# Three plain chunks instead of four, then halves of 448 columns, with part of the softmax on ScalarE

## The chip, the cores and the metric

One core of a Trainium2 chip runs the whole kernel. The metric is the device time of one execution in microseconds: 953.92 us is the median of 3 runs of the kernel before (953.56 to 955.15). PE is TensorE, PEld its weight loads, DVE is VectorE, ACT is ScalarE, POOL is GpSimd, SP is SyncE.

## The reference

Sliding-window attention over 8 batches, 8 heads, 576 positions of width 64, then a gated feed-forward layer on the 4608 x 512 result:

```python
scores = scale * np.matmul(q, k.transpose(0, 1, 3, 2))
mask_plain = (rel >= 0) & (rel < 32)                       # heads 0 to 3
mask_dil = (rel >= 0) & (rel < 128) & (rel % 4 == 0)       # heads 4 to 7
scores = np.where(masks, scores, -1000000000.0)
scores = scores - np.max(scores, axis=-1, keepdims=True)
attn = np.exp(scores)
attn = attn / (np.sum(attn, axis=-1, keepdims=True) + 1e-09)
x = matmul(attn, v)   # brought to [4608 tokens, 512]
g = x @ w_gate        # 512 x 1536
silu = g * (1.0 / (1.0 + np.exp(-g)))
out = (silu * (x @ w_val) @ w_out)                         # 1536 x 512
```

## The kernel before, in words

Tokens are cut into 12 chunks of 384 (`CH`). Attention works on packs: a pack is a pair of heads in a chunk, so there are 48, m = 0 to 47, four to a chunk. Each query block of 32 sees only 64 keys, so a pack is three or four groups of 128 queries by 64 keys for two heads.

A pack is handled in two visits, placed by the table `visit` (filled by `visits`) between the matmul groups of the feed-forward layer. Visit A of pack m (`attend`) issues the value matmuls of pack m - 1 (`results`), the score matmuls of m, then on DVE the normalising of m - 1 (`norm`) and the mask sum, maximum and subtraction of m (`shift`), on ACT the exponential (`exps`), and the loads of later packs on ACT's queue. Visit B transposes the normalised result of m - 1 (`turn_y`) and the exponentials of m (`turn_e`) on PE, copies both out of PSUM on ACT, and so gives four packs' worth of x for a chunk. Both visits use the one PSUM tile `two`.

The feed-forward layer has three parts. Every fp32 operand is split into a rounded high part and a rest (both float32r), and a product is high x high + high x low + low x high, three matmuls.

- Plain stage: the first 4 chunks (`NPLAIN`), each in 12 steps s over blocks of 128 of the 1536 columns. A step is 12 gate matmuls into `bank_g`, 12 value matmuls into `bank_v` (`gv_mm`), and 12 output matmuls of the step before (`out_mm`). ACT takes the tanh (`act_tanh`), DVE two products (`dve_u`, `dve_h`), ACT the high part (`h_hi`), POOL the rest (`h_lo`). During the first chunk the weights are loaded and decoded from 64-bit words.
- Mixing: in steps 12 to 47 sums and differences of weight blocks are made for the last stage (18 mixes, one for each i and `which`): `mix_parts` and `mix_sums` on DVE, a cast on ACT, `mix_low` on DVE, then four DMA to the DRAM tile `pieces` (`mix_out`); unmixed blocks go there directly (`plain_parts`).
- Halved stage: the other 8 chunks, two at a time (ci = 0 to 3). A pair is multiplied as 2 x 2 blocks with seven products instead of eight. `x_step` makes the seven x operands from the four quarters of x (two halves of tokens b11/b12, b21/b22) for the next pair at the end of the pair before; `gate_val` does 6 matmuls for each of 7 products, 6 blocks, gate and value; `gated` combines them; `h_split` makes the seven hidden operands; `outs` does 3 matmuls for each of 7 products, 6 blocks, 2 rows; `out_done` stores. The weight pieces come back from DRAM through a ring of 10 buffers (`ask`, on POOL's queue). The line L739 is every matmul of this stage, L698 is every subtraction or sum made through the helper `tt`.

The order of instructions on an engine is not that of the text: a scheduler of the framework places each instruction where it expects it ready, by program order as priority; `issue_after` and `manual_schedule` bind it in places. Within an engine the placed order is then kept.

## Time and profile before

| | |
|---|---|
| median of the runs | 953.92 us |
| profiled execution | 953.3 us |
| its span | 951.4 us |
| PE busy | 939.0 us |
| DVE busy | 653.7 us |
| ACT busy | 406.6 us |
| POOL busy | 376.8 us |
| DMA, mean over the span | 250 GB/s |

Busy time is the union of an engine's instructions in one profiled execution. Matmuls are pipelined: a row's mean duration (336 ns for 384 columns) is longer than the distance between the starts of two, and it is the distance that fills the span.

### The profile page before, as it was taken

How to read it: one execution, taken by the hardware profiler on the slowest of the kernel's cores; microseconds unless marked ns; L12 is line 12 of the kernel's file. 1: busy time of each engine (PE TensorE's matmuls, PEld its weight loads, DVE VectorE, ACT ScalarE, POOL GpSimd, SP SyncE). 2: the span in 40 equal slices, each digit the busy share in tenths (PEclk: the TensorE clock that was granted, in tenths of full speed). 3: DMA queues.
4: the chain of work that ended last, by engine and by line, in shares of the span. 5: the costliest groups of instructions: out<-in, count | busy, mean ns of one | idle time of the engine just before them, and what ended most of it. 6: DMA issues, size and time to landing. Idle time of an engine off the chain costs nothing.

```text
span 951.4 us, 23933 instructions
## 1 busy us (share of the span) xinstructions
PE 939.0 (99%) x9960; PEld 914.2 (96%) x9960; DVE 653.7 (69%) x1168; ACT 406.6 (43%) x788; POOL 376.8 (40%) x460
## 2 busy tenths in 40 slices
PE   7899999999999999999999999999999999999998
PEld 5799999999999999999999999999999999999998
DVE  4766557677667654776887677789487779466583
ACT  4886322333334223434454344446334446234352
POOL 1766311211111222343276334366244448354472
PEclk9999999999999999999999999999999999999999
DMA  9975164665766882989888988888989878988873
GB/s 368 339 281 188 43 218 154 241 205 201 240 233 224 270 293 70 279 272 297 270 271 275 330 287 258 270 254 291 350 262 297 244 237 281 309 245 261 250 235 120
DMA packets 86060, 238.12 MB, mean 250 GB/s; under 512 B 8768, under 2 KB 29120, under 8 KB 85952
## 3 DMA queue, kind: packets, MB, share of 16 engines
q0 software_dynamic: 36288, 132.14, 44.5%
q1 hardware_dynamic: 36848, 65.07, 19.4%
q10 hardware_dynamic: 12816, 39.38, 12.3%
q8 instruction: 79, 1.29, 0.5%
q14 instruction: 29, 0.24, 0.1%
HBM read 194.08 MB, written 42.47 MB: 249 GB/s over the span
## 4 chain that ended last, share of the span: by engine, by line
PE 93%; DVE 4%; ACT 2%; issue 1%; DMA 0%; ACTq 0%; DVEq 0%
PE bo L739 31%; PE bg L739 11%; PE bv L739 11%; PE bo L465 10%; PE bv L428 10%; PE bg L428 10%; PE two L366 3%; PE two L326 3%; PE two L350 2%; PE two L384 2%; DVE at_float32r L698 1%; DVE at_float L698 0%; DMA at_bfloat<-masks 0%; ACT at_float32r L246 0%; ACT at_int L207 0%
## 5 line engine op out<-in xcount | busy, mean ns | idle before, releaser
L739 PE MATMUL bo<-at_float32r,at_float32r 128*128 128x384 f32 x1728 | 318.6, 336 | 0.0
L739 PEld LDWEIGHTS bo<-at_float32r,at_float32r 128*128 128x128 f32 x1728 | 299.7, 188 | 1.1
L671 POOL DMA_DIRECT2D at_float32r<-pieces x252 | 137.8, 547 | 245.0 <-PE bo L739 140.5
L698 DVE TENSOR_TENSOR at_float<-bo,at_float 128x384 f32<-128x384 f32 x224 | 122.2, 553 | 101.7 <-PE bo L739 52.4
L457 POOL TENSOR_TENSOR at_float32r<-at_float,at_float32r 128x384 fp32r<-128x384 f32 x48 | 55.6, 1158 | 216.5 <-PE bo L465 169.5
L739 PE MATMUL bg<-at_float32r,at_float32r 128*128 128x384 f32 x648 | 137.0, 336 | 0.0
L739 PE MATMUL bv<-at_float32r,at_float32r 128*128 128x384 f32 x648 | 136.4, 336 | 0.0
L739 PEld LDWEIGHTS bv<-at_float32r,at_float32r 128*128 128x128 f32 x648 | 114.0, 188 | 0.5
L739 PEld LDWEIGHTS bg<-at_float32r,at_float32r 128*128 128x128 f32 x648 | 113.7, 188 | 0.7
L428 PE MATMUL bg<-at_float32r,at_float32r 128*128 128x384 f32 x576 | 111.5, 340 | 2.1 <-DVE at_float L442 1.4
L728 ACT CAST at_float32r<-at_float 128x384 fp32r<-128x384 f32 x168 | 82.9, 513 | 66.8 <-PE bv L739 22.7
L698 DVE TENSOR_TENSOR at_float32r<-at_float,at_float32r 128x384 fp32r<-128x384 f32 (+1 forms) x112 | 99.1, 908 | 17.9 <-ACT at_float32r L728 14.0
L428 PE MATMUL bv<-at_float32r,at_float32r 128*128 128x384 f32 x576 | 110.8, 339 | 0.0
L465 PE MATMUL bo<-at_float32r,at_float32r 128*128 128x384 f32 x576 | 109.4, 337 | 0.0
L698 POOL TENSOR_TENSOR at_float32r<-at_float,at_float32r 128x384 fp32r<-128x384 f32 x84 | 91.6, 1091 | 43.9 <-ACT at_float32r L728 42.8
L428 PEld LDWEIGHTS bg<-at_float32r,at_float32r 128*128 128x128 f32 x576 | 100.3, 188 | 3.9 <-POOL at_float32r L250 1.1
L428 PEld LDWEIGHTS bv<-at_float32r,at_float32r 128*128 128x128 f32 x576 | 100.4, 188 | 0.9
L465 PEld LDWEIGHTS bo<-at_float32r,at_float32r 128*128 128x128 f32 x576 | 100.4, 188 | 0.5
L765 ACT ACTIVATE at_float<-at_float 128x384 f32<-128x384 f32 x96 | 50.6, 527 | 99.4 <-DVE at_float L698 92.3
L442 DVE SCALAR_TENSOR_TENSOR at_float<-at_float,bg 128x384 f32<-128x384 f32 x48 | 26.6, 554 | 77.6 <-ACT at_float L437 77.6
L744 ACT COPY at_float<-bg 128x384 f32<-128x384 f32 x84 | 40.1, 478 | 81.4 <-PE bg L739 81.2
L698 DVE TENSOR_TENSOR at_float<-at_float,at_float 128x384 f32<-128x384 f32 (+1 forms) x64 | 54.6, 878 | 25.1 <-POOL at_float32r L698 11.3
(80 smaller groups left out, 987.8 us busy)
## 6 DMA issues: line engine op xcount, KB each, us to landing
at_float32r<-pieces POOLq DMA_DIRECT2D x252, 512.0 KB, 4.8
pieces<-at_float32r SPq DMA_DIRECT2D x126, 256.0 KB, 3.3
at_int<-w SPq DMA_DIRECT2D x24, 768.0 KB, 6.1
at_float<-vb ACTq DMA_DIRECT2D x36, 390.0 KB, 5.2
out<-at_float SPq DMA_DIRECT2D x48, 192.0 KB, 4.1
at_float<-qkb ACTq DMA_DIRECT2D x14, 448.0 KB, 6.1
at_float<-qkb ACTq DMA_DIRECT2D x15, 400.0 KB, 5.5
at_float<-qkb ACTq DMA_DIRECT2D x7, 640.0 KB, 7.0
```

Source lines behind the costliest of these rows:

```text
L326: nc.tensor.matmul(out=two[BQ * j:BQ * j + BQ, h, a + BK * g:a + BK * g + BK], lhsT=t[r, q:q + BQ], rhs=t[r, k:k + BK], start=not masked, ...
L366: nc.tensor.matmul(out=two[BQ * j:BQ * j + BQ, h, (D + 1) * g:(D + 1) * (g + 1)], lhsT=t[r, BQ * i:BQ * i + BQ], rhs=v[r, i, :], start=Tru ...
L428: nc.tensor.matmul(out=bank[:, :CH], lhsT=wcol(f, o, low), rhs=x[ORDER[j]], start=n == 0, stop=n == len(ops) - 1)
L442: last["h"] = nc.vector.scalar_tensor_tensor(out=t, in0=t, scalar=1.0, in1=bank_g[:, :CH], op0=ALU.add, op1=ALU.mult)
L457: nc.gpsimd.tensor_tensor(out=hl, in0=hst[i][0], in1=hst[i][1], op=ALU.subtract)
L465: nc.tensor.matmul(out=bank_o[j][:, :CH], lhsT=wcol(f, 2 * DM + P * j, low), rhs=x, start=f == 0 and low == 0 and x is hh, stop=f == NF - ...
L671: nc.gpsimd.dma_start(out=taken[asked], in_=pieces[asked % NPIECE])
L698: engine.tensor_tensor(out=out, in0=a, in1=b, op=op)
L728: nc.scalar.copy(out=o[:, 0], in_=src)
L739: nc.tensor.matmul(out=bank, lhsT=w, rhs=x, start=first and n == 0 and t in FRESH, stop=last and n == len(ops) - 1, skip_group_check=True)
L744: nc.scalar.copy(out=kept[KEPT[t]][r], in_=banks[0][r][:, :CH])
L765: nc.scalar.activation(out=f, in_=g, func=AF.Tanh, scale=0.5)
```

## The change

There are three plain chunks. The remaining 9 chunks of tokens are worked through in four pairs of halves, 448, 448, 448 and 384 wide (`HCS`), whose starts no longer coincide with the chunks of attention. So a pack's x goes out in pieces (`x_copies`), and what belongs to the pair after the one being filled goes to a spill buffer and is copied back later (`x_spilt`). The first difference of x is made in place of its first quarter (`x1 = b11`), and the two differences of hidden blocks are made in place on POOL after the first split. The buffers are laid out anew: the ring of pieces has 9, the hidden splits run 8 ahead, not 10.

In packs 9 to 23 (`by_group`) DVE only scales the maximum; ACT subtracts it as the bias of the exponential, one instruction for each group and head (64 columns), and does the division by the sum the same way. The 24 packs that the first pair needs now stand in three chunks' steps. The 18 mixes stand in steps 12 to 32, in four named places of a step, with two output buffers. Plain chunks are stored from ACT's queue, not SP's.

```diff
-NPLAIN = 4
+NPLAIN = 3
+HCS = (448, 448, 448, 384)
+HM = max(HCS)
...
+    def by_group(m):
+        return 8 < m < 24
...
+        if by_group(m):
+            nc.vector.tensor_scalar(out=mx, in0=mx, scalar1=-0.125, scalar2=None, op0=ALU.mult)
+            st[m]["bias"] = mx
+            return
         nc.vector.tensor_tensor(out=ev, in0=s, in1=mx.unsqueeze(3).broadcast_to([P, 2, ng, BK]), op=ALU.subtract)
...
+        for g in range(pk(m).ng):
+            for h in range(2):
+                nc.scalar.activation(out=e[:, g, h], in_=e[:, g, h], func=AF.Exp, scale=0.125,
+                                     bias=st[m]["bias"][:, h, g:g + 1])
...
+        if by_group(m):
+            for g in range(ng):
+                for h in range(2):
+                    nc.scalar.activation(out=y[:, g, h], in_=s[:, h, g, :D], func=AF.Copy, scale=z[:, h, g:g + 1])
+            return
...
-            nc.sync.dma_start(out=out[P * j:P * j + P, CH * ci:CH * ci + CH], in_=ot)
+            nc.scalar.dma_start(out=out[P * j:P * j + P, CH * ci:CH * ci + CH], in_=ot)
...
+    for n in range(8):
+        visits(9 + n, NB + 2 + 4 * n, NB + 5 + 4 * n)
+        visits(17 + n, SB - 38 + 4 * n, SB - 35 + 4 * n)
...
+    for m in range(32, NPK + 1):
+        a = SB + NSLOT * (m // 8 - 3) - 32 + (m % 8 > 0) * 6 + 15 * (m % 8)
         visits(m, a, a + 7)
...
+    mix_at = {NF + n * 20 // (3 * NP - 1): n for n in range(3 * NP)}
...
-    NAT = 10
+    NAT = 9
...
+        if ci > 0:
+            steps = [steps[k] for k in (0, 2, 6, 8, 3, 4, 5, 1, 7, 9, 10)]
...
         act_tanh(s)
+        mix_one(mix_high, mix_at.get(s - 1), "t")
         attend(3 * s)
         dve_u(s)
-        mix_to(2 * (s - NF) + 1)
+        plain_to(s - 10)
+        mix_one(mix_low, mix_at.get(s - 1), "h")
+        mix_one(mix_out, mix_at.get(s - 1), "w")
+        mix_one(mix_parts, mix_at.get(s), "h")
...
         dve_h(s)
+        mix_one(mix_sums, mix_at.get(s), "h")
         h_hi(s)
```

How it moves instructions, at three places. First PE in the halved stage, gate and value matmuls of one block (`bg`, `bv`, `bo` are the PSUM banks; the last field is partitions x columns). Before:

```order
L739 MATMUL bv<-at_768_float32r,at_1024_float32r 128x384 x6
L739 MATMUL bo_503<-at_768_float32r,at_1024_float32r 128x384 x6
L739 MATMUL bo_507<-at_768_float32r,at_1024_float32r 128x384 x6
L739 MATMUL bg<-at_768_float32r,at_1024_float32r 128x384 x6
L739 MATMUL bv<-at_768_float32r,at_1024_float32r 128x384 x6
```

Of the change:

```order
L799 MATMUL bv<-at_896_float32r,at_1024_float32r 128x448 x6
L799 MATMUL bo_503<-at_896_float32r,at_1024_float32r 128x448 x6
L799 MATMUL bo_507<-at_896_float32r,at_1024_float32r 128x448 x6
L799 MATMUL bg<-at_896_float32r,at_1024_float32r 128x448 x6
L799 MATMUL bv<-at_896_float32r,at_1024_float32r 128x448 x6
```

The sequence is the same, each matmul is 64 columns wider; 2268 matmuls have 448 columns and 2052 have 384, where 4752 had 384.

Second ACT in the plain stage, from one visit of a pack to the next (L356 and L381 copy the keys' transposes, L403 and L436 the high part of x, L437 and L488 are the tanh, L452 and L503 the cast `h_hi`, L629 and L680 the mixing's cast, L346 and L370 the exponential, L406 the scaling). Before:

```order
L308 DMA at_780_float_891<-vb 128x780
L302 DMA at_1280_float_516<-qkb 128x800
L452 CAST at_384_float32r<-at_384_float_586 128x384
L346 ACTIVATE at_384_float_887<-at_384_float_887 128x384
L629 CAST at_2048_float32r<-at_1024_float_518 128x4x256
L437 ACTIVATE at_384_float_630<-bg 128x384
L452 CAST at_384_float32r<-at_384_float_630 128x384
L356 COPY at_384_float_954<-two 128x384
L403 CAST at_384_float32r<-two 128x384
```

Of the change:

```order
L318 DMA at_780_float_884<-vb 128x780
L312 DMA at_1280_float_516<-qkb 128x896
L406 ACTIVATE at_384_float_1078<-two,at_6_float_298 128x64 x6
L503 CAST at_384_float32r<-at_384_float_623 128x384
L488 ACTIVATE at_384_float_579<-bg 128x384
L680 CAST at_2048_float32r<-at_1024_float_518 128x4x256
L370 ACTIVATE at_384_float_880<-at_384_float_880,at_6_float_237 128x64 x6
L503 CAST at_384_float32r<-at_384_float_579 128x384
L381 COPY at_384_float_947<-two 128x384
L436 CAST at_384_float32r<-two 128x384
```

Twelve instructions of 64 columns stand where one of 384 stood, and the exponentials stand behind a tanh and a mixing cast.

Third PE in the same stretch, from the matmuls ahead of a pack's visit B to its transposes, in the change from the scores (L341) on (L384 and L414 transpose the result, L350 and L375 the exponentials). Before:

```order
L465 MATMUL bo_511<-at_384_float32r,at_1536_float32r 128x384
L465 MATMUL bo_515<-at_384_float32r,at_1536_float32r 128x384
L428 MATMUL bg<-at_384_float32r,at_1536_float32r 128x384 x12
L428 MATMUL bv<-at_384_float32r,at_1536_float32r 128x384 x12
L384 MATMUL two<-at_256_float_59,at_384_float_1085 128x128 x3
L350 MATMUL two<-at_256_float_59,at_384_float_887 128x128 x3
L465 MATMUL bo_503<-at_384_float32r,at_1536_float32r 128x384 x2
```

Of the change:

```order
L341 MATMUL two<-at_1280_float_516 32x64 x24
L516 MATMUL bo_507<-at_384_float32r,at_1536_float32r 128x384
L516 MATMUL bo_511<-at_384_float32r,at_1536_float32r 128x384
L516 MATMUL bo_515<-at_384_float32r,at_1536_float32r 128x384
L479 MATMUL bg<-at_384_float32r,at_1536_float32r 128x384 x12
L479 MATMUL bv<-at_384_float32r,at_1536_float32r 128x384 x12
L414 MATMUL two<-at_256_float_59,at_384_float_1078 128x128 x3
L516 MATMUL bo_503<-at_384_float32r,at_1536_float32r 128x384 x2
L375 MATMUL two<-at_256_float_59,at_384_float_880 128x128
L516 MATMUL bo_507<-at_384_float32r,at_1536_float32r 128x384 x2
L375 MATMUL two<-at_256_float_59,at_384_float_880 128x128
```

The transposes of the exponentials, three in a piece before, now stand one by one between output matmuls.

## Rows read from the trace of the kernel before

**Rows 1.** The page, busy time, share of the span and instructions of each engine.

```profile
PE 939.0 (99%) x9960; PEld 914.2 (96%) x9960; DVE 653.7 (69%) x1168; ACT 406.6 (43%) x788; POOL 376.8 (40%) x460
```

**Rows 2.** The chain that ended last, whole span, shares by engine and line.

```profile
by line: PE bo L739 30.7%; PE bg L739 11.3%; PE bv L739 11.3%; PE bo L465 10.2%; PE bv L428 10.2%; PE bg L428 10.1%; PE two L366 2.8%; PE two L326 2.5%; PE two L350 1.6%; PE two L384 1.5%; DVE at_float32r L698 1.2%; issue 0.8%; DVE at_float
```

**Rows 3.** Two windows: PE, PEld, DVE, ACT, POOL busy us; clock, DMA share, GB/s.

```profile
150.00:340.00 190.00, 190.00 (x2329) 185.09 (x2328) 133.10 (x261) 61.81 (x113) 34.52 (x35) 1.00 0.68 231
400.00:900.00 500.00, 499.93 (x4952) 491.39 (x4951) 364.15 (x645) 220.80 (x460) 234.57 (x328) 1.00 0.88 277
```

**Rows 4.** PE's timeline, halved stage: start us, us, what; first and eleventh group.

```profile
798.45 0.69 PE L739 MATMUL bv<-at_float32r,at_float32r 128*128 128x384 f32 x3
...
803.65 0.68 PE L739 MATMUL bv<-at_float32r,at_float32r 128*128 128x384 f32 x3
```

**Rows 5.** Groups of instructions by form, PE: count, busy us, mean ns, idle before.

```profile
L739 PE MATMUL bo<-at_float32r,at_float32r 128*128 128x384 f32 x1728 | 318.6, 336 | 0.0
...
L739 PE MATMUL bg<-at_float32r,at_float32r 128*128 128x384 f32 x648 | 137.0, 336 | 0.0
...
L428 PE MATMUL bg<-at_float32r,at_float32r 128*128 128x384 f32 x576 | 111.5, 340 | 2.1 <-DVE at_float L442 1.4 <-POOL at_float32r L250 0.8
```

**Rows 6.** The same view, DVE: a step's product, mixing, softmax.

```profile
L442 DVE SCALAR_TENSOR_TENSOR at_float<-at_float,bg 128x384 f32<-128x384 f32 x48 | 26.6, 554 | 77.6 <-ACT at_float L437 77.6
...
L632 DVE TENSOR_TENSOR at_float32r<-at_float,at_float32r 128x1024 fp32r<-128x1024 f32 x18 | 23.6, 1313 | 7.0 <-ACT at_float32r L629 7.0
...
L341 DVE TENSOR_TENSOR at_float<-at_float,at_float 128x384 f32<-128x384 f32 x34 | 20.7, 608 | 0.6
L377 DVE TENSOR_TENSOR at_float<-two,at_float 128x384 f32<-128x384 f32 x36 | 20.1, 557 | 1.2
...
L340 DVE TENSOR_REDUCE at_float<-at_float 128x6 f32<-128x384 f32 x34 | 18.7, 551 | 0.9
L338 DVE TENSOR_TENSOR at_float<-two,at_bfloat 128x384 f32<-128x384 f32 x34 | 18.6, 548 | 0.0
...
L619 DVE TENSOR_TENSOR at_float<-at_float32r 128x512 f32<-128x512 f32 x24 | 15.4, 684 | 0.0
...
L619 DVE TENSOR_TENSOR at_float<-at_float32r 128x256 f32<-128x256 f32 x24 | 8.6, 418 | 0.0
L627 DVE TENSOR_TENSOR at_float<-at_float 128x256 f32<-128x256 f32 x18 | 8.5, 470 | 0.5
...
L375 DVE TENSOR_SCALAR at_float<-two 128x6 f32<-128x6 f32 x36 | 5.7, 158 | 14.9 <-PE two L326 14.9
```

**Rows 7.** The same view, ACT: tanh, exponential, mixing's cast, copy out of PSUM.

```profile
L437 ACT ACTIVATE at_float<-bg 128x384 f32<-128x384 f32 x48 | 23.5, 489 | 62.6 <-PE bg L428 58.1 <-DMA at_float<-vb 4.5
...
L346 ACT ACTIVATE at_float<-at_float 128x384 f32<-128x384 f32 x40 | 20.9, 523 | 36.0 <-DVE at_float L341 36.0
L629 ACT CAST at_float32r<-at_float 128x1024 fp32r<-128x1024 f32 x18 | 18.9, 1049 | 19.4 <-DVE at_float L628 19.0 <-DMA pieces<-at_float32r 0.4
L356 ACT COPY at_float<-two 128x384 f32<-128x384 f32 x36 | 17.2, 478 | 14.8 <-PE two L350 13.9
...
L346 ACT ACTIVATE at_float<-at_float 128x512 f32<-128x512 f32 x8 | 5.1, 632 | 8.3 <-DVE at_float L341 8.3
```

**Rows 8.** Timelines of DVE and of POOL in the plain stage.

```profile
150.21 0.56 DVE L442 SCALAR_TENSOR_TENSOR at_float<-at_float,bg 128x384 f32<-128x384 f32 x1 [1.50 <-ACT at_float L437]
150.68 1.22 DVE L632 TENSOR_TENSOR at_float32r<-at_float,at_float32r 128x1024 fp32r<-128x1024 f32 x1
...
159.82 2.02 DVE L632 TENSOR_TENSOR at_float32r<-at_float,at_float32r 128x1024 fp32r<-128x1024 f32 x1 [1.25 <-ACT at_float32r L629]
...
159.74 1.01 POOL L457 TENSOR_TENSOR at_float32r<-at_float,at_float32r 128x384 fp32r<-128x384 f32 x1 [5.30 <-PE bo L465]
```

**Rows 9.** Timelines near the end of the second pair: DVE, then PE.

```profile
650.54 8.12 DVE L698 TENSOR_TENSOR at_float32r<-at_float,at_float32r 128x768 fp32r<-128x768 f32 x7
...
661.96 0.55 PE L350 MATMUL two<-at_float,at_float 128*128 128x128 f32 x3
```

More of the change, by code (lines that the diff above doesn't have):

```diff
@@ L36 @@
 BK = 2 * BQ
-NPLAIN = 4
-CC = 2 * CH
+NPLAIN = 3
+HCS = (448, 448, 448, 384)
+HM = max(HCS)
+STARTS = [CH * NPLAIN + 2 * sum(HCS[:n]) for n in range(len(HCS) + 1)]
 NT = 7
@@ L109, in attention_moe @@
     NCH = out.shape[1] // CH
+    NC = len(HCS)
+    assert STARTS[NC] == out.shape[1]
     NS = NPLAIN * NF
@@ L405, in x_copies, with x_spilt @@
         else:
-            x = x32_first[k // 2] if c == NPLAIN else x32[k // 2][c % 2]
-            src, x = x_views(m, bank, x[:, k % 2, :])
-            nc.scalar.copy(out=x, in_=src)
-        st[m].clear()
+            n = len(SEGMENTS[c % 3]) if pk(m).ng * P > CH else 1
+            ahead = sum(CH * c >= x for x in STARTS)
+            for g in range(n):
+                a, t, left = pk(m).ng * P // n * g, CH * c + CH // n * g, CH // n
+                while left:
+                    ci = sum(t >= x for x in STARTS) - 1
+                    h, r = divmod(t - STARTS[ci], HCS[ci])
+                    w = min(left, HCS[ci] - r)
+                    x = x32[k // 2][h][:, k % 2, r:r + w]
+                    if ci == ahead:
+                        x = spill[k // 2][:, k % 2, r:r + w]
+                        spilt[ci] = max(spilt.get(ci, 0), r + w)
+                    nc.scalar.copy(out=x, in_=bank[:, a:a + w])
+                    a, t, left = a + w, t + w, left - w
+        st[m].clear()
+    def x_spilt(ci):
+        n = spilt.pop(ci, 0)
+        if n:
+            for a in range(2):
+                nc.scalar.copy(out=x32[a][0][:, :, :n], in_=spill[a][:, :, :n])
     def x_copy_hi(m, bank):
@@ L436, in act_tanh @@
         t = t_ring()
[L437 removed]
+        last["t"] = nc.scalar.activation(out=t, in_=bank_g[:, :CH], func=AF.Tanh, scale=0.5)
         hst[i] = [t, None, None]
@@ L640, in mix_out, with mix_one, plain_to @@
             last["w"] = nc.sync.dma_start(out=pieces[p, :, o:o + 4 * P], in_=t[:, k].rearrange("p l c -> p (l c)"))
-    mixed = 0
-    def mix_stage():
-        nonlocal mixed
-        n, stage = divmod(mixed, 3)
-        mixed += 1
-        if n < 3 * NP:
-            with tc.issue_after(last["h"].ins):
-                (mix_parts, mix_sums, mix_low)[stage](n)
-            with tc.issue_after(last["w"].ins):
-                if stage == 0:
-                    plain_parts(*divmod(n, 3))
-                elif stage == 2:
-                    mix_out(n)
-    NAT = 10
+    mix_at = {NF + n * 20 // (3 * NP - 1): n for n in range(3 * NP)}
+    def mix_one(what, n, behind):
+        if n is not None:
+            with tc.issue_after(last[behind].ins):
+                what(n)
+    plain = 0
+    def plain_to(n):
+        nonlocal plain
+        while plain < min(n, 3 * NP):
+            with tc.issue_after(last["w"].ins):
+                plain_parts(*divmod(plain, 3))
+            plain += 1
     taken = {}
     asked = 0
-    NC = (NCH - NPLAIN) // 2
     def ask(n):
@@ L740, in products, with keep, total @@
                              stop=last and n == len(ops) - 1, skip_group_check=True)
-    def keep(t, r):
+    def keep(t, r, hc):
         if t in KEPT:
-            nc.scalar.copy(out=kept[KEPT[t]][r], in_=banks[0][r][:, :CH])
-    def total(t, r, ring):
+            nc.scalar.copy(out=kept[KEPT[t]][r][:, :hc], in_=banks[0][r][:, :hc])
+    def total(t, r, ring, hc):
         _, b, k = SUMS[t]
-        o = ring()
-        tt(nc.vector, o, banks[b][r][:, :CH], kept[k][r], ALU.add)
+        o = ring()[:, :hc]
+        tt(nc.vector, o, banks[b][r][:, :hc], kept[k][r][:, :hc], ALU.add)
         return o
@@ L786, in out_done @@
             a, b = SUMS[t][0]
-            o = total(t, r, o_ring)
-            row, col = P * (2 * a + r), CH * (NPLAIN + 2 * ci + b)
-            nc.sync.dma_start(out=out[row:row + P, col:col + CH], in_=o)
-    def mix_to(half):
-        while mixed < half * 9 * NP // 62:
-            mix_stage()
+            o = total(t, r, o_ring, HCS[ci])
+            row, col = P * (2 * a + r), STARTS[ci] + HCS[ci] * b
+            nc.sync.dma_start(out=out[row:row + P, col:col + HCS[ci]], in_=o)
     for s in range(NS):
```

149 lines of the change are left out of this document (76 added, 73 removed).

## The prediction

> **What bounds the kernel now.** I read the page's busy shares first, then the chain of waits, then two windows, then single lines. The page has TensorE (PE) busy for 939.0 of 951.4 us [rows 1], and the chain that ended last, followed back, runs through PE matmuls for over 90% of the span: 83.8% in the big matmuls of L739, L428 and L465 together, 8.4% (2.8 + 2.5 + 1.6 + 1.5) in the attention's small ones, 79.9 us for 44 packs, 1.8 us each [rows 2]. In the plain stage (150 to 340 us) PE is busy for 190.00 of 190.00 us while VectorE (DVE) has 133.10 (70%) and ScalarE (ACT) 61.81; in the halved stage (400 to 900 us) PE has 499.93 of 500, DVE 364.15, ACT 220.80 [rows 3]. The granted clock is 1.00 in both, the 2.4 GHz level. So the time is the number of matmuls times their spacing, and every other engine matters only where PE has to wait for it. The spacing is in the timeline: ten groups of three L739 matmuls start between 798.45 and 803.65, 5.20 us for 30, 173.3 ns each [rows 4]. 384 columns at 2.4 GHz are 160.0 ns, so 13.3 ns lie beside the columns. The counts are 1728 + 648 + 648 = 3024 in the halved stage and 576 each of gate, value and output, 1728, in the plain one [rows 5] (the value's and the plain output's rows have the same counts).
>
> **The change: fewer, wider matmuls.** A plain chunk takes 12 x 36 = 432 matmuls, a halved one 7 x 6 x 2 x 6 + 7 x 6 x 2 x 3 = 756. Before: 4 x 432 + 4 x 756 = 4752, all of 384 columns. After: 3 x 432 + 756 = 2052 of 384, and 3 x 756 = 2268 of 448. So 432 go: 432 x 0.1733 = -74.9 us. 2268 grow by 64 columns. The trace has no matmul of 448 columns, so the price is bounded. Below: the columns alone, 448 / 2.4 = 186.7 ns, +13.4 each, +30.4 us. Above: the whole spacing grows in proportion, 173.3 x 448 / 384 = 202.2 ns, +28.9 each, +65.5 us. I take 173.3 + 64 / 2.4 = 200.0 ns, the 13.3 ns staying what they are per matmul, since these ns belong to each row of [rows 4] whatever stands before it: +26.7 each, +60.5 us. Net -14.4 us, with ends of -44.5 and -9.4.
>
> The Trainium skill (TensorE: Matmul & The Clock Gate, Back-to-back issue gap) gives an isolated gap of N/2.4 + 2.5 ns. That is an estimate of 162.5 ns for 384 columns, and the trace does not agree: it has 173.3. By that formula 448 columns take 189.2 ns, and the whole step saves 432 x 162.5 ns less 2268 x 26.7 ns, 9.7 us in place of 14.4.
>
> **What is unchanged on PE.** All 48 packs, the first chunk's weight decoding and the order of PE up to step 12 are the same, and the last halved chunk has 384 columns as before, so the end is too. 24 packs stood before the halved stage and 24 do now; their 1.8 us each move, they do not grow.
>
> **The added work on ACT and its wait.** Packs 9 to 23 lose the subtraction (608 ns) and the scaling (557 ns) on DVE and gain a 128x6 scaling (158 ns) [rows 6]: 15 x 1.0 = 15 us less on DVE. On ACT one exponential of 384 becomes six of 64, and six scaled copies come. The rows have 523 ns for 384 and 632 for 512 columns of exponential, 0.85 ns a column and 196 ns fixed, so 251 ns for 64; a copy out of PSUM takes 478 for 384, so with the same slope and fixed part about 0.21 [rows 7]. Per pack ACT goes from 0.52 to 1.51 + 1.28 = 2.8 us, 15 x 2.3 = 34 us more, on an engine with two thirds of its time free there [rows 3].
>
> These operations stand in queues. The rows of order in the change's section show one such pack: on ACT the six copies, a hidden-layer cast, the tanh of a step, the mixing's cast, then the six exponentials; on PE 3 + 12 + 12 + 2 = 29 matmuls and three transposes (5.0 + 0.3 = 5.4 us) between its scores and the first transpose of its exponentials. The tanh can't start before the twelve gate matmuls in front of it end, 15 x 0.1733 = 2.6 us after the scores. Then tanh 0.49, mixing cast 1.05, two exponentials 0.50: ready 4.6 us after the scores, wanted at 5.4. DVE's mask sum 0.55, maximum 0.55, the product behind the tanh 0.55 and the scaling 0.16 end at 3.8, so ACT is last. Spare: 0.7 us, and behind the waiting exponentials stand the next cast of the hidden layer and the copies of the keys, on which PE's results wait. Before, one exponential stood there and the subtraction ran on DVE: PE takes its three transposes in one piece there, now one by one.
>
> Price of that wait: at least nothing, since such chains ended in time in the whole plain stage before [rows 3]. At most the whole lengthening of the chain on each of 16 visits: exponentials +0.98, copies ahead of them 1.28, scaling +0.16, less 0.61 and 0.56 on DVE, 1.25 us, 20 us. I take 2.5 us, near the lower end, because the worked pack has 0.7 us to spare and because a late exponential delays PE once and gives ACT the same time to catch up.
>
> **The mixing in 20 steps.** One mix on DVE is two sums of 684 or four of 418 ns, four differences of up to 470, one 1313: 4.6 us [rows 6], 18 of them 83 us. With 24 x 2 x 0.55 for the hidden layer (L442's time twice), 16 packs x 1.6 (mask sum, maximum, two small ops and a scaling), the first halved chunk's 11 steps on x at 1.16 x 7/6 and copies, DVE has 26 + 83 + 26 + 15 + 4 = 154 us in steps 12 to 35. PE has 24 x 36 x 0.1733 + 16 x 1.8 = 179. So 86%, against 70% now, and single durations overlap by some 0.09 us (a row of 0.56 is followed 0.47 later [rows 8]), so rather 80. It still hides, but with less room: I count its part in the 2.5 us. Stores of the plain chunks move from SP's to ACT's queue, 12 issues, each behind a copy on DVE or ACT; next in line is a tanh with four matmul groups' time before the bank is wanted. Nothing counted. Writes of the pieces: 126 x 256 KB in some 165 us, beside the packs' loads about 280 GB/s, as much as is moved in the halved stage now [rows 3].
>
> One rule speaks against this packing. The row shows the 1024-wide difference of the mixing at 1.22 us, and at 2.02 us when it starts 0.08 us behind a GpSimd subtraction of 1.01 us that runs beside it [rows 8]. The Trainium skill (SBUF — State Buffer, Who interferes with whom) says that a DVE operation with two SBUF inputs and a GpSimd operation that reads SBUF exclude each other for the whole instruction. The trace agrees, with 0.80 us lost.
>
> **The halved stage.** DVE's and PE's work grow alike (448/384 = 1.167 against 200.0/173.3 = 1.154), so DVE's 73% stays. The ring of pieces shrinks from ten to nine: lead 9 x 12 x 0.2 = 21.6 us against 20.8. Splits of the hidden layer run 8 instead of 10 ahead: 8 x 6 x 0.2 = 9.6 us against 10.4. The tight place is the chunk's end, where seven splits of x hold DVE for 8.12 us and a pack's transposes start at 661.96 close behind its exponential [rows 9]. That pack now comes six places later, and the x work spreads as before. Nothing counted; a hundred ns either way.
>
> **Sum.** The profiled execution took 953.3 us (951.4 span + 1.9 around it); 953.3 - 14.4 + 2.5 = 941.4. The median of the runs lies 0.6 above that execution: 942.0.
>
> **Rivals.** (a) The wider matmul costs other than by the column. For: no 448 in the trace. At 186.7 ns: 953.9 - 44.5 + 2.5 = 912. Against it: the 13.3 ns are there in every group. At 202.2: 953.9 - 9.4 + 2.5 = 947.
>
> By the formula of the Trainium skill named above the same place gives 953.9 - 9.7 + 2.5 = 946.7, which falls into the dear end of (a).
>
>  (b) The exponentials in pieces make PE wait at every pack. For: 0.7 us of room, and six operations in a row behind a tanh; against: ACT is only a third busy. At 0.96 us a pack, 15 packs, the gain is gone: 954. (c) Slower: DVE becomes the bound of steps 12 to 35. Its place is the mixing, its price the exclusion of [rows 8]: if all mixing operations are stretched as 2.02 to 1.22, 83 us become 137, DVE has 208 against PE's 179, and the time is 953.9 - 14.4 + 29 = 968. It decides from a stretch of 30% (25 of 83 us). Against: the means used already include such meetings, and GpSimd has one operation of 1.0 to 1.2 us a step there. That the change doesn't do what it says is ruled out: the order shows 2268 matmuls of 448 columns.
>
> **How the numbers follow.** Forecast, 938 to 947: 0.68. (a) cheap 0.05, dear 0.09. (b) 947 to 955: 0.10. (c) 0.08. No change is within 0.2%, 1.9 us, about what a measurement of this kernel can tell: 952.0 to 955.8. (b) puts 0.04 there and 0.06 below. Faster 0.68 + 0.05 + 0.09 + 0.06 = 0.88, taken as 0.87; same 0.04; slower 0.09. The range leaves out (a) cheap, (c) and the end of (b): 936.5 to 952.
>
> **What will show it.** The spacing of the 448-wide matmuls (200 ns right, below 190 or above 203 wrong). In the plain stage: PE's waits on the exponentials (total under 5 us right, over 12 wrong), DVE under 90% there. At the ends of the halved chunks: no wait of PE over 1 us. A total saving of PE's busy time unlike 14 us would make the sum wrong; a saving as forecast with the time unchanged would mean (b) or (c).

## The result, and the profile after

The changed kernel takes 958.2 us (median of 6 runs, 957.8 to 960.5) where the kernel before has 954.2: ratio 1.0044, 95% interval 1.0031 to 1.0057. It is 0.4% slower, and I had forecast 942.0. The profiled execution is the slowest of the six: 960.5 us with a span of 958.6, 2.3 us above the median. Before it was 953.3 and 951.4, 0.9 us below the median. The page's first line, which answers to [rows 1]:

```profile
PE 939.6 (98%) x9528; PEld 869.4 (91%) x9528; DVE 672.0 (70%) x1123; ACT 451.2 (47%) x965; POOL 380.9 (40%) x448
```

432 matmuls fewer, and PE is busy as long as before (939.6 against 939.0). Two stretches of the changed kernel, columns as in [rows 3]:

```profile
150.00:340.00 190.00, 186.18 (x2440) 172.77 (x2439) 135.59 (x265) 103.39 (x293) 36.07 (x44) 1.00 0.79 265
400.00:900.00 500.00, 500.00 (x4314) 460.26 (x4313) 363.61 (x568) 214.09 (x421) 229.77 (x294) 1.00 0.79 246
```

In the halved stage PE is full, as before. In the plain stage it has 186.18 of 190 us, where it had all. DVE is at 135.59 of 190 (71%; before 133.10), ACT at 103.39 (before 61.81). Two rows of PE's timeline in the halved stage, which answer to [rows 4], the first and the tenth of groups of three matmuls, now of 448 columns:

```profile
445.23 0.78 PE L799 MATMUL bg<-at_float32r,at_float32r 128*128 128x448 f32 x3
...
450.79 0.78 PE L799 MATMUL bv<-at_float32r,at_float32r 128*128 128x448 f32 x3
```

Nine groups of three start in 5.56 us, 27 matmuls of 205.9 ns. Over all 2268 of them the mean from start to start is 204.9 ns, with waits behind a matmul counted apart (0.3 ns more or less by where the line to a wait is drawn). My sum had 200.0. Groups by form, as in [rows 5 to 7]:

```profile
L799 PE MATMUL bo<-at_float32r,at_float32r 128*128 128x448 f32 x1296 | 281.4, 369 | 0.0
L799 PE MATMUL bg<-at_float32r,at_float32r 128*128 128x448 f32 x486 | 117.7, 368 | 0.0
L375 PE MATMUL two<-at_float,at_float 128*128 128x128 f32 x140 | 27.8, 282 | 6.0 <-ACT at_float L370 3.0 <-ACT at_float L366 2.1
L375 PEld LDWEIGHTS two<-at_float,at_float 128*128 128x128 f32 x140 | 17.3, 141 | 11.9 <-ACT at_float L370 7.0 <-ACT at_float L366 3.3
L370 ACT ACTIVATE at_float<-at_float,at_float 128x64 f32<-128x64 f32 x94 | 24.1, 336 | 20.7 <-DVE at_float L358 16.6 <-DMA out<-at_float 3.9
L406 ACT ACTIVATE at_float<-two,at_float 128x64 f32<-128x64 f32 x94 | 20.9, 324 | 36.9 <-DVE at_float L401 30.4 <-issue 6.5
L684 DVE TENSOR_TENSOR at_float32r<-at_float,at_float32r 128x1024 fp32r<-128x1024 f32 x18 | 22.0, 1223 | 5.0 <-ACT at_float32r L680 4.3 <-DMA pieces<-at_float32r 0.5
```

L370 are the exponentials in pieces, L366 those in one piece, L375 the transposes of both on PE and L406 the scaling.

The sequence of starts on PE divides the span. The distances from one big matmul's start to the next add up to 829.3 us before (4751 of 174.5 ns) and 825.7 after: 2051 of 384 columns at 175.9 and 2268 of 448 at 204.9. That is -3.6 us in place of -14.4. Stalls, the time that a start lies behind where the matmul before it let it be, grew by 10.7 us in place of 2.5. 953.3 - 3.6 + 10.7 = 960.4, the profiled time. The small attention matmuls took the same 77 us. The medians are only 4.0 us apart, so with the same spacing the stalls of a median execution grew by some 7.6 us. And 1.6 us of the 10.7 lie outside the stretch that the change repacks: between 60 and 100 us PE has 38.37 of 40 us (before 40.00), behind a load of weights that ACT waits for:

```profile
92.89 0.93 ACT L217 ACTIVATE at_int<-at_int 128x768 f32<-128x768 f32 x1 [4.50 <-DMA at_int<-w]
```

### The profile page after: what moved, and what is told of

The parts are those of the page before. It is cut to its first block, busy times and chain, and to the rows that moved or that the text cites. A ratio compares the mean times of both kernels' runs of the same rounds, so it can differ in the third digit from the quotient of the medians.

```text
span 958.6 us, 23201 instructions
## 1 busy us (share of the span) xinstructions
PE 939.6 (98%) x9528; PEld 869.4 (91%) x9528; DVE 672.0 (70%) x1123; ACT 451.2 (47%) x965; POOL 380.9 (40%) x448
## 4 chain that ended last, share of the span: by engine, by line
PE 79%; DVE 6%; DMA 5%; ACT 4%; issue 2%; SPq 1%; ACTq 0%; DVEq 0%
PE bo L799 36%; PE bg L799 13%; PE bv L799 13%; DMA pieces<-at_float32r 3%; PE bo L516 3%; PE bv L479 3%; PE bg L479 3%; PE two L391 2%; PE two L341 2%; DVE at_float32r L684 1%; PE two L375 1%; DMA at_int<-w 1%; PE two L414 1%; SPq L692 1%; ACT at_float L370 1%
## 5 line engine op out<-in xcount | busy, mean ns | idle before, releaser
L799 PE MATMUL bo<-at_float32r,at_float32r 128*128 128x448 f32 (+1 forms) x1728 | 360.0, 361 | 0.0
L748 DVE TENSOR_TENSOR at_float<-bo,at_float 128x448 f32<-128x448 f32 (+1 forms) x224 | 134.3, 604 | 138.2 <-PE bo L799 72.8
L799 PE MATMUL bg<-at_float32r,at_float32r 128*128 128x448 f32 (+1 forms) x648 | 151.8, 360 | 0.0
L799 PE MATMUL bv<-at_float32r,at_float32r 128*128 128x448 f32 (+1 forms) x648 | 151.6, 360 | 0.0
L748 DVE TENSOR_TENSOR at_float32r<-at_float,at_float32r 128x448 fp32r<-128x448 f32 (+3 forms) x112 | 121.4, 1106 | 22.0 <-ACT at_float32r L784 14.6
L748 POOL TENSOR_TENSOR at_float32r<-at_float,at_float32r 128x448 fp32r<-128x448 f32 (+1 forms) x84 | 106.1, 1263 | 49.8 <-ACT at_float32r L784 48.7
L508 POOL TENSOR_TENSOR at_float32r<-at_float,at_float32r 128x384 fp32r<-128x384 f32 x36 | 39.2, 1090 | 168.8 <-ACT at_float32r L503 83.4
L479 PE MATMUL bg<-at_float32r,at_float32r 128*128 128x384 f32 x432 | 86.8, 345 | 2.6 <-DVE at_float L493 1.9
L479 PE MATMUL bv<-at_float32r,at_float32r 128*128 128x384 f32 x432 | 85.0, 341 | 0.0
L516 PE MATMUL bo<-at_float32r,at_float32r 128*128 128x384 f32 x432 | 84.7, 343 | 0.0
```

The costliest lines, as they stand in the source:

```text
L479: nc.tensor.matmul(out=bank[:, :CH], lhsT=wcol(f, o, low), rhs=x[ORDER[j]], start=n == 0, stop=n == len(ops) - 1)
L508: last["l"] = nc.gpsimd.tensor_tensor(out=hl, in0=hst[i][0], in1=hst[i][1], op=ALU.subtract)
L516: nc.tensor.matmul(out=bank_o[j][:, :CH], lhsT=wcol(f, 2 * DM + P * j, low), rhs=x, start=f == 0 and low == 0 and x is hh, stop=f == NF - ...
L748: engine.tensor_tensor(out=out, in0=a, in1=b, op=op)
L799: nc.tensor.matmul(out=bank, lhsT=w, rhs=x, start=first and n == 0 and t in FRESH, stop=last and n == len(ops) - 1, skip_group_check=True)
```

## Experiments on the spacing

**Matmuls alone.** A kernel of blocks of 96 matmuls, one line of code a block:

```diff
+    xs = [ops[:, X0 + 512 * n + x_off:X0 + 512 * n + x_off + width] for n in range(4)]
+    ws = [ops[:, W0 + 256 * n + w_off:W0 + 256 * n + w_off + P] for n in range(4)]
...
+        for a in block(448):
+            nc.tensor.matmul(**a)
```

> Nothing but blocks of 96 float32r matmuls one behind the other with no other engine at work (attention, weights' decoding, mixing and stores of results are left out); blocks differ in the columns, and for some in where the operands stand in SBUF. Theory (width and place): 448 columns take 204 ns from start to start here too, not 200.0, and 384 take 173.3 where the moving operand starts on a multiple of 64 bytes, 176 where it starts 32 bytes behind one (448: 204 and 205). Rival (crowding): the spacing of 448 is stretched by what the other engines and the DMA do to SBUF; here it is 200.0 or the columns alone (186.7 to 189), and the 32 bytes change nothing.

Rows of its timeline (start, length, line, form, count); from one block's start to the next one's there are 96 spacings:

```profile
91.79 16.80 PE L161 MATMUL b<-at_float32r 128*128 128x384 f32 x96
108.43 0.88 PE L163 MATMUL b<-at_float32r 128*128 128x400 f32 x4
```

```profile
263.24 21.92 PE L179 MATMUL b<-at_float32r 128*128 128x512 f32 x96
285.00 1.22 PE L181 MATMUL b<-at_float32r 128*128 128x256 f32 x9
```

384 columns: 16.64 us / 96 = 173.3 ns. 512: 21.76 / 96 = 226.7. Both are the columns plus 13.3 ns, my rule, and so are 400 (180.0) and 496 (220.0). In between they are dearer: 416 188.3, 432 195.7, 448 202.7 in its first block, 464 209.0, 480 216.8, up to 3.5 ns over the rule. So width matters on an otherwise idle core, and the extra does not need crowding. But later blocks of 448 had 200.0 (moving operands 64 bytes further on), 204.4 (weights 32 bytes further on) and 206.6. 384 columns took 176.6 with the moving operands shifted by 32 bytes, and 173.6 with the weights shifted along. So place matters too, and a shift of 32 bytes is not the rule. By the formula of the Trainium skill (TensorE: Matmul & The Clock Gate, Back-to-back issue gap) 448 columns are estimated at 189.2 ns; the measurement does not agree, its lowest block had 200.0.

**All buffers on 64 bytes, and four halves of 432.** Two edits of the changed kernel:

```diff
-    M_ATT = M_SMALL + 40
+    M_ATT = M_SMALL + 48
```

```diff
-HCS = (448, 448, 448, 384)
+HCS = (432, 432, 432, 432)
...
-    SPILL = 256
+    SPILL = 288
```

> The changed kernel, all buffers behind the small ones 32 bytes further up, so that all moving operands of the big matmuls start on multiples of 64 bytes. Theory (place): plain output matmuls 177 to 173.4 ns (432), the gate and value matmuls of the second chunk 176 to 173.4 (288), the last pair's outputs 176.3 to 173.4 (252), the 448-wide outputs 205.1 to 204.2 (756): 1.6 + 0.7 + 0.7 + 0.7 = 3.7 us less, 954.5 where the changed kernel has 958.2. Rival: the levels of 173 and 176 belong to the stretch and not to the place, time unchanged at 958.2.

956.4 us (ratio to before 1.0023, 1.001 to 1.0036): half of the gain expected. The 448s fell from 204.9 to 204.5 ns, the 384s from 175.9 to 175.4.

> The changed kernel with four pairs of halves of 432 columns in place of 448, 448, 448, 384 (and a spill buffer of 288 in place of 256): the same columns and the same number of matmuls. By my prediction's rule (13.3 ns and the columns) the sum over a set of four is the same (3 x 200.0 + 173.3 = 773.3 against 4 x 193.3), so the time would stay at 958.2. Theory (width has its own price): the block of 432 took 195.7 to 196.7, so 756 x (4 x 196.2 - 3 x 204.9 - 176) = -4.7 us, time 953.5.

955.9 us (1.0025, 1.0016 to 1.0034). The 432s took 196.5 ns; a set of four took 786 ns, where three of 448 and one of 384 took 791. Right in sign, half in size, and still no gain over before.

**A map of places.** As the first kernel, with the four moving operands adjacent as in the halved stage, shifted against the weights:

```diff
+        for a in block(448, x_off=16):
+            nc.tensor.matmul(**a)
```

> Again only blocks of 96 float32r matmuls with nothing else at work (all of the kernel's own computation is left out), the four moving operands now adjacent as in the halved stage, shifted by multiples of 64 bytes against the weights. Theory (phase): the spacing is N + 32 columns at best (200.0 for 448, 193.3 for 432), and for 416 to 480 columns the place of the operands decides whether 0 to 16 columns' time comes on top; so 448 shows several levels between 200.0 and 206.7 by the shift, and each shift shows the same level when it is repeated later. 496 and 504 columns stand at the best level (220.0, 223.3). Rival (memory of what ran before): the level changes between two blocks of the same shift.

Blocks of 448 columns shifted by 0, 64, 128 and 192 bytes, and two shifted by 32 bytes (in the second the weights with them):

```profile
33.78 19.61 PE L152 MATMUL b<-at_float32r 128*128 128x448 f32 x96
53.24 19.37 PE L154 MATMUL b<-at_float32r 128*128 128x448 f32 x96
72.44 19.74 PE L156 MATMUL b<-at_float32r 128*128 128x448 f32 x96
92.03 19.57 PE L158 MATMUL b<-at_float32r 128*128 128x448 f32 x96
111.44 0.77 PE L160 MATMUL b<-at_float32r 128*128 128x448 f32 x3
```

```profile
455.00 20.00 PE L196 MATMUL b<-at_float32r 128*128 128x448 f32 x96
474.84 20.00 PE L198 MATMUL b<-at_float32r 128*128 128x448 f32 x96
494.67 5.64 PE L200 MATMUL b<-at_float32r 128*128 128x448 f32 x27
```

In order: 202.7, 200.0, 204.1, 202.2 ns, then 206.7 and 206.6. Shifts of 256, 512 and 1024 bytes gave 202.7 like 0; shifting the weights by 64 or 128 bytes gave 202.2 and 203.9, as 192 and 128 of the operand do; a shift repeated 600 us later gave its first level to 0.1 ns. So for shifts by multiples of 64 bytes the place decides, counted between weights and moving operand, in steps that repeat every 256 bytes; the rival, memory of what ran before, falls for these. It is not the whole rule. The second block shifted by 32 bytes has the same distance between weights and operand as the first block of all, and took 206.6 ns, not 202.7. In the first kernel of matmuls alone, blocks at distance 0 that used one PSUM bank only, one block of weights, one moving operand or other output columns took 206.6 or 206.7, too. What sets these stays open. Two parts of the theory missed: 496 and 504 columns took 223.4 and 228.7 ns, not 220.0 and 223.3, and 432 columns took 195.5 to 197.8 at every shift tried, not 193.3.

By the addresses of the built program, 1692 of the changed kernel's 2268 matmuls of 448 columns stood 0 bytes behind a multiple of 256 and 576 stood at 96. From start to start they took 204.3 and 205.3 ns in its trace, so at 0 some 1.6 ns more than alone, which is not explained.

**The buffers moved, nothing else.** The order on each engine is the same in both kernels:

```diff
-    M_ATT = M_SMALL + 40
+    M_ATT = M_SMALL + 80
...
-    NSPARE = 1448
+    NSPARE = 1408
...
-    M_RING = M_W + NT * 4 * HM
-    M_HQ = M_RING + NAT * PIECE
+    M_RING = M_W + NT * 4 * HM + 48
+    M_HQ = M_RING + NAT * PIECE + 16
```

> The changed kernel with buffers shifted by 16 to 80 columns, nothing else: the order on every engine is the same. The moving operands of the halved stage now start 64 bytes behind a multiple of 256 bytes counted from the weights' place, where blocks of 448 took 200.1 ns alone, in place of 0 (202.7 alone, 204.2 in the kernel) and of other places (205.1). All other moving operands start on multiples of 256 bytes. Theory (the place sets the spacing): 1512 x 3 + 756 x 4 ns = 7.6 us and up to 2 us on the matmuls of 384 less, time 949 to 952. Rival (what else runs sets it): spacing at 204 to 205 as before, 958.2.

948.4 us (0.9942, 0.9929 to 0.9955): 9.8 us less than the changed kernel, and faster than the kernel before. The same rows of the timeline as above:

```profile
444.97 0.76 PE L799 MATMUL bg<-at_float32r,at_float32r 128*128 128x448 f32 x3
...
449.17 0.77 PE L799 MATMUL bv<-at_float32r,at_float32r 128*128 128x448 f32 x3
```

Seven groups, 21 matmuls, in 4.20 us: 200.0 ns. All 2268 now stand at 64 bytes. The distances of the big matmuls sum to 813.3 us, 15.9 less than before, where I had -14.4. The stalls did not fall.

**The same for the kernel before** (`M_ATT` and `NSPARE` as in the diff above):

> The kernel before with the same shift of buffers (the second x buffer and one of ten buffers of hidden splits move to a multiple of 256 bytes; the others stood on one already). Theory (the place sets the spacing): 576 gate and value matmuls and some 100 output matmuls go from 176 to 173.4 ns, -1.8 us, 952.2; so the change, both kernels well placed, is worth 948.4 - 952.2 = -3.8 us, and not -14.4 + 2.5. Rival (places matter only at 448 columns): unchanged, 953.9 to 954.2.

952.0 us (0.9976, 0.9967 to 0.9985), near what was expected. With both kernels well placed the change is worth 948.4 - 952.0 = -3.6 us.

## Experiments on the waits of the plain stage

PE's waits of the changed kernel in 100 to 310 us (line, releaser, us, times, longest); before, this view is empty there:

```profile
PE two L375 <- ACT at_float L370: 3.0, 5, 1.2
PE bg L479 <- DVE at_float L493: 0.5, 1, 0.5
PE two L391 <- DVE at_float32r L437: 0.3, 1, 0.3
```

One pack of it, first PE, then DVE, then ACT:

```profile
203.40 0.49 PE L414 MATMUL two<-at_float,at_float 128*128 128x128 f32 x3
205.11 0.33 PE L375 MATMUL two<-at_float,at_float 128*128 128x128 f32 x1 [1.22 <-ACT at_float L370]
```

```profile
199.32 0.16 DVE L400 TENSOR_SCALAR at_float<-two 128x6 f32<-128x6 f32 x1
199.44 0.69 DVE L668 TENSOR_TENSOR at_float<-at_float32r 128x512 f32<-128x512 f32 x1
200.05 0.18 DVE L401 RECIPROCAL at_float<-at_float 128x6 f32<-128x6 f32 x1
200.15 0.65 DVE L668 TENSOR_TENSOR at_float<-at_float32r 128x512 f32<-128x512 f32 x1
...
201.97 0.68 DVE L353 TENSOR_TENSOR at_float<-two,at_bfloat 128x512 f32<-128x512 f32 x1
202.57 0.85 DVE L676 TENSOR_TENSOR at_float<-at_float 128x256 f32<-128x256 f32 x1
203.35 0.67 DVE L355 TENSOR_REDUCE at_float<-at_float 128x8 f32<-128x512 f32 x1
203.94 0.41 DVE L677 TENSOR_TENSOR at_float<-at_float 128x256 f32<-128x256 f32 x1
204.28 0.16 DVE L358 TENSOR_SCALAR at_float<-at_float 128x8 f32<-128x8 f32 x1
```

```profile
200.26 1.34 ACT L406 ACTIVATE at_float<-two,at_float 128x64 f32<-128x64 f32 x6 [2.12 <-DVE at_float L401]
...
204.47 1.78 ACT L370 ACTIVATE at_float<-at_float,at_float 128x64 f32<-128x64 f32 x7 [2.46 <-DVE at_float L358]
```

The six exponentials begin at 204.47; PE wanted the first at 203.9. The links of the softmax are L400, L401, then ACT's scaling, on which DVE's L353 waits (12.2 us in all by its group), L355 and L358, and operations of the mixing (L668 to L677) stand between them. My prediction had the scaling of the maximum (L358) end before the exponentials' turn on ACT, "so ACT is last"; here ACT waits 2.46 us for it. Before, the division was DVE's own and the mixing spread over 36 steps.

Two rows of ACT's waits from 100 to 312 us belong to its own DMAs. Each of these three waits, 10.4 us in all, holds stores or loads that ACT issues just ahead of the softmax's instruction ("issue" is a wait for which the profile names no releaser):

```profile
ACT at_float L406 <- issue: 6.5, 2, 3.7
ACT at_float L370 <- DMA out<-at_float: 3.9, 1, 3.9
```

**Softmax back on DVE,** whole, or the division alone:

```diff
-        return 8 < m < 24
+        return False
```

> The changed kernel with the subtraction of the maximum and the division back on DVE in one operation each, for all packs. Theory (round trips): the waits of PE behind small matmuls and behind big ones in the plain stage come from the division on ACT, which sends each pack from DVE to ACT to DVE to ACT; without it they fall by about 7 us of the 10.7, time 951 us. Rival (DVE crowded): the 15 us that DVE takes back in steps 12 to 35 beside the mixing and 16 packs make the waits larger, 962 or more. Second rival: visits too close in a pack, time unchanged at 958.

956.9 us (1.0029, 1.0018 to 1.0041), 1.3 us below the changed kernel, which is near the spread of its runs. The division alone:

```diff
-        if by_group(m):
+        if False:
             for g in range(ng):
```

> The changed kernel with only the division back on DVE (one product of 384 columns); the subtraction stays in ACT's exponentials. Theory (round trips): this alone removes the step DVE - ACT - DVE ahead of the mask's sum, time 953 us, most of what undoing both gives. Rival (the six exponentials hold up PE): time within 1.5 us of 958.2.

961.8 us (1.0077, 1.006 to 1.0093). Neither theory holds: the pieces on ACT are worth 1.3 us at most, and half of them is worse than all. In the first of the two PE's stalls move from the exponentials to the results (L391 behind the copies that empty the PSUM tile).

**Without the mixing's arithmetic; stores on SP:**

```diff
     def mix_sums(n):
-        a11, a12, a21, a22 = halves(n)
...
+        pass
```

(`mix_parts`, `mix_high` and `mix_low` are emptied in the same way, and `mix_out` writes four pieces straight from a block of weights.)

> The changed kernel without the mixing's arithmetic: no sums, differences and casts on DVE and ACT; the same pieces are written, but from unmixed weights. Theory (mixing in 20 steps fills DVE's queue so that a pack's next link comes late): the waits of PE in the plain stage fall from some 10 us to the 3 of before, time 951. Rival (packs too close together): 16 packs in 24 steps with one place between a pack's second visit and the next pack's first make PE wait by themselves, time within 2 us of 958.2.

961.6 us (1.0085, 1.0069 to 1.0101): slower with 72 us less work on DVE. Its waits of ACT at 100 to 340 us, and the place of the largest, by windows:

```profile
ACT at_float L406 <- DMA pieces<-at_float32r: 19.3, 5, 6.5
ACT at_float L370 <- DMA out<-at_float: 9.7, 1, 9.7
```

```profile
118.00:125.00 7.00, 7.00 (x130) 6.66 (x129) 3.13 (x8) 0.75 (x2) 1.00 (x1) 1.00 1.06 379
125.00:132.00 7.00, 3.70 (x16) 2.66 (x15) 1.11 (x2) 2.25 (x8) 0.00 (x0) 0.81 1.02 349
132.00:139.00 7.00, 7.00 (x120) 6.47 (x120) 1.50 (x5) 1.59 (x5) 1.01 (x1) 0.70 1.05 369
```

ACT's own DMA issues hold it. In the trace all DMAs that ACT and SP issue report their landing on the same eight semaphores, in turn. A load or store that ACT issues first waits for the DMA that had its semaphore before, mostly a piece of the mixing that SP sent. Two loads in the built program of the changed kernel (the `DMAHW` are the eight, here for the buffer's last load and the semaphore's last use):

```
L318 DMA at1928_780_float32_884<-vb 128x780 [waits DMAHW7_49,DMAHW2_49,PE_49]
L312 DMA at648_1280_float32_516<-qkb 128x800 [waits DMAHW5_49,DMAHW1_49,PE_49]
```

Without arithmetic the pieces go out earlier and denser (DMA share 1.06, 1.02 and 1.05 in these windows, where the changed kernel has 0.32, 0.66 and 1.01), and behind the waiting issue stand the scaling and the exponentials.

The stores back on SP, with the mixing:

```diff
-            nc.scalar.dma_start(out=out[P * j:P * j + P, CH * ci:CH * ci + CH], in_=ot)
+            nc.sync.dma_start(out=out[P * j:P * j + P, CH * ci:CH * ci + CH], in_=ot)
```

> The changed kernel with the plain chunks stored from SP's queue again. Theory: the issues of the stores hold ACT for 1 to 2 us once in a chunk with a pack's scaling behind them (PE lost 0.8 us near 227 us), so 1 to 2 us less, 956.5 to 957. Rival: on SP's queue they stand behind the mixing's pieces and hold the banks' copies, time unchanged or longer.

959.2 us (1.0058, 1.0041 to 1.0074): no gain. On SP's queue the stores wait for the copies on ACT (42.6 us in three pieces), and ACT still waits around its loads (3.9, 2.3 and 1.7 us ahead of three scalings).

**Loads elsewhere, the chain first, and both causes away:**

```diff
-                load_v(m, later, nc.scalar)
+                queue = nc.gpsimd if 8 < m < 24 else nc.scalar
+                load_v(m, later, queue)
...
-                    load_qk(m + 1, later, nc.scalar)
+                    load_qk(m + 1, later, queue)
```

> The changed kernel, the loads of packs in the plain stage (packs 9 to 23) issued from POOL's queue in place of ACT's. Theory (ACT held by its own DMA issues: each issue waits for the eighth DMA before it, mostly a slow piece of the mixing, and the softmax's operations stand behind it): PE's stalls fall by 3 to 5 us, time 954. Rival (DVE's order alone): the stalls stay near 10 us, time within 1.5 us of 958.2.

972.1 us (1.019, 1.0172 to 1.0207): far worse. Its largest stall:

```profile
231.27 0.49 PE L414 MATMUL two<-at_float,at_float 128*128 128x128 f32 x3
238.29 1.43 PE L375 MATMUL two<-at_float,at_float 128*128 128x128 f32 x3 [6.53 <-ACT at_float L370]
```

```profile
224.04 3.86 ACTq L526 DMA_DIRECT2D out<-at_float  x4
...
235.23 1.04 ACT L681 CAST at_float32r<-at_float 128x1024 fp32r<-128x1024 f32 x1 [4.86 <-issue]
237.65 2.02 ACT L370 ACTIVATE at_float<-at_float,at_float 128x64 f32<-128x64 f32 x8 [1.37 <-DVE at_float L358]
```

```profile
236.31 1.23 DVE L685 TENSOR_TENSOR at_float32r<-at_float,at_float32r 128x1024 fp32r<-128x1024 f32 x1 [4.54 <-ACT at_float32r L681]
237.45 0.17 DVE L358 TENSOR_SCALAR at_float<-at_float 128x8 f32<-128x8 f32 x1
```

The mixing's cast on ACT (L681) waits 4.86 us for its output buffer. The wait is for the plain chunk's four stores (L526), not for pieces of the mixing: the change lays the second of the two mixing buffers where the stores are read from (both start at `M_OUT`), and by the trace's semaphores the wait ends at 235.16, when the last of the stores lands, 7.9 us after its issue. DVE's difference (L685) waits for the cast, and the softmax's scaling L358 stands behind it: PE loses 6.53 us. A mix bound into DVE's queue passes the landing of DMAs on to the softmax. In the changed kernel this wait for the stores is 1.4 us; a run with a separate buffer was not made.

The chain first (the mixing's sums are placed behind the instruction that `last["h"]` names):

```diff
-            nc.vector.tensor_scalar(out=mx, in0=mx, scalar1=-0.125, scalar2=None, op0=ALU.mult)
+            last["h"] = nc.vector.tensor_scalar(out=mx, in0=mx, scalar1=-0.125, scalar2=None, op0=ALU.mult)
...
+        if m > 8:
+            last["h"] = o
```

> The changed kernel with the mixing's sums bound behind the softmax's last DVE operation of the pack at hand, where the scheduler had put them between its links (the mask's sum, the maximum, the scaling). Theory (mixing between the links): from 199.3 to 204.4 us five of DVE's seven links' idle places hold mixing, 3 us in each pack; with the chain in one piece the stalls of 190 to 300 us fall from 9 to 3 us, time 952. Rival (ACT's DMA issues): 957 to 958.

> As the kernel with the mixing behind the chain, and with the subtraction and the division whole on DVE. Theory (mixing between the links): the chain of a pack is in one piece on DVE and 1 us shorter over ACT; 951 or less. Rival (DVE too full without ACT's help): later than the kernel with the chain first alone, 956 or more.

957.2 us (1.0033, 1.002 to 1.0046) and 956.6 (1.0032, 1.0017 to 1.0046). The sums between the links are not it: moving them behind gains nothing that can be told.

> Without the mixing's arithmetic (the pieces hold unmixed weights) and with the packs' loads on POOL's queue. Theory (two causes, mixing between the links and ACT held at its DMA issues): with both taken away the plain stage has no more stalls than before, 3 us, time 951, though without mixing alone the time was 961.6. Rival (packs too close together): stalls of 6 us or more stay, 955 or more.

954.2 us (1.0008, 0.9999 to 1.0018), between theory and rival. From 150 us on PE is full; one stall stays near 128 us, where ACT waits 10.2 us behind the stores.

> The changed kernel with the loads of packs 9 to 23 and the stores of the plain chunks on SP's queue: ACT issues no DMA in the plain stage, and POOL none either. Theory (ACT held at its DMA issues): the stalls in the plain stage fall from 10 to 6 us, time 954. Rival (the loads come too late behind the mixing's pieces, as they did from POOL's queue): 962 or more. Second rival (ACT's issues cost nothing): 958.

> Without the mixing's arithmetic (the pieces hold unmixed weights), the packs' loads on POOL's queue and the plain chunks' stores on SP's. Theory: the one stall that was left in this family, 5.6 us at 120 to 140 us, is ACT held for 10 us behind the first chunk's stores; it goes, time 949 to 950. Rival (it belongs to the first mixes or to the packs): 954.

With the mixing, loads and stores on SP give 966.8 us (1.0127, 1.0112 to 1.0141), the time of the first rival. But its reason is not shown: neither here nor with the loads on POOL's queue does PE wait for a load. Without the mixing's arithmetic, loads on POOL and stores on SP give 948.4 (0.9939, 0.9926 to 0.9952), and the plain stage's window is full:

```profile
100.00:340.00 240.00, 240.00 (x3121) 229.59 (x3120) 99.82 (x207) 112.69 (x336) 64.83 (x87) 1.00 0.74 253
```

So the packs are not too close together: with the mixing's arithmetic and ACT's loads and stores both away nothing is left of the plain stage's stall. Without the arithmetic ACT's loads are worth 961.6 - 954.2 = 7.4 us and its stores 954.2 - 948.4 = 5.8. With it, moving them made the kernel slower (972.1 for the loads on POOL, 966.8 for both on SP), and those two runs put new work into other queues, so they do not price ACT's issues by themselves. What the mixing and ACT's issues are each worth in the changed kernel, and why the loads on POOL's queue cost so much with the mixing, stays open beyond the one stall shown.

**Both improvements together,** then the mixes over 22 steps:

```diff
-    mix_at = {NF + n * 20 // (3 * NP - 1): n for n in range(3 * NP)}
+    mix_at = {NF + n * 22 // (3 * NP - 1): n for n in range(3 * NP)}
```

> The buffers shifted as in the kernel before this, the mixing behind the softmax's chain, subtraction and division whole on DVE. If the place is worth 7 us and the rest the 1.6 us that it was worth by itself: 948, faster than both kernels. If the place is worth nothing: 956.6.

946.7 us (0.9921, 0.9908 to 0.9934): the fastest of all, 7.5 us below the kernel before and 5.3 below it with its buffers well placed.

> The kernel with shifted buffers, the mixing behind the chain and the softmax whole on DVE, and the 18 mixes over 22 steps in place of 20. Theory (DVE's operations of the mixing are what the packs wait for): 10% fewer mixes beside a pack, 1 to 2 us less than 946.7. Rival (the mixes' end collides with the first operations on x for the halved stage): 1 to 3 us more.

949.8 us (0.9955, 0.994 to 0.9969): the rival. PE waits 4.8 us in one piece behind the last plain chunk's copies on ACT, at the passage to the halved stage.

## Why the prediction was wrong, point by point

- **Counts and what bounds the kernel: right.** 432 matmuls went, 2268 widened, PE is still the bound.
- **The step that failed first: "I take 173.3 + 64 / 2.4 = 200.0 ns".** It measured 204.9, 11.1 us over 2268 matmuls. The 13.3 ns do not belong to a matmul as such: at 448 columns they are 13.3 to 20 ns, and where the weights and the moving operand stand moves them. [Rows 4] showed one place, the best one. In the kernel before, the gate and value matmuls of one plain chunk in two stood at another (176.6 ns on the mean, against 173.6) in the same trace; reading the spacing stage by stage would have shown it. With buffers moved the 200.0 came out to a tenth.
- **The 384s: not foreseen.** The new layout put more of them at worse places, 174.5 to 175.9 ns on the mean, 2.9 us. Against a mean of 174.5 before, the 448s cost 30.4 ns more and not 26.7 (8.4 us); with 0.5 us more for those removed, 8.4 + 2.9 - 0.5 = 10.8 us, the gap between -14.4 and -3.6.
- **The second step that failed: waits at 2.5 us, "near the lower end".** They were 10.7 in the profiled execution, some 7.6 by the medians. I had worked one pack by its links on ACT, with "ACT is last", and counted the mixing only by its length. I had "nothing counted" for the stores and for the denser pieces. With the mixing's arithmetic and ACT's loads and stores away the stalls were gone; so the softmax was held behind DMA issues on ACT and behind the mixing, whose cast and difference can wait for landings. Their shares are open. My test, PE's waits on the exponentials under 5 us in the plain stage, was met (3.0 us in 100 to 310 us) and still misled: PE's row has 6.0 us in all in front of these transposes, but the weight loads' row has 11.9.
- **Rivals.** (a), dear, was right in kind, and 204.9 lies beyond its 202.2, the end that I had taken for the highest. (b) comes near the stalls' size, 10.7 us against 14.4, but not their cause: the pieces on ACT are worth 1.3 us at most. (c) is refuted as it was priced: DVE is at 71%, and the mixing's difference took 1223 ns on the mean (before 1313), so it was not stretched. The mixing has its part in the stalls all the same. No rival had dear matmuls and stalls together, which is what came.
- **Durations and the halved stage: right.** Six exponentials took 1.54 us (worked 1.51), six scalings 1.34 (1.28), and PE has 500.00 of 500 us.

## What to carry to other kernels

Before a matmul's width is priced, measure its spacing alone, at the places in SBUF and with the PSUM banks that it will have, and keep the offset between weights and moving operand one of those measured as good. Where an engine issues DMAs, count each issue as an instruction that can wait for a DMA of another queue, and ask what stands behind it. Two uses of one buffer tie their queues together; look for such pairs when a layout is made anew. A mean over a kernel's rows hides levels: look at the same matmul in each stage.

## What was not expected of the hardware

- At 448 columns, alone on the core: 200.0 to 206.7 ns, with the same level again at shifts of 256, 512 and 1024 bytes between weights and moving operand; 384, 400, 496 and 512 columns reach columns plus 13.3 ns too (496 in another block took 223.4, 512 with a shift of 32 bytes 233.4), while no block of 416, 432, 464 or 480 did.
- In the run without the mixing's arithmetic, the granted clock was 0.81 in the window where PE had 3.70 of 7 us, and 0.70 in the next, where PE is full: behind the wait it ran for a stretch at the lower of its levels, 1.2 GHz (twelve matmuls took 4.21 us in place of 2.28). This stall was paid twice.
